# Grouped weight transfers, a hand-ordered SyncE queue and a new attention timetable in a three-stage mixer kernel

## The chip, the cores and the metric

The kernel runs on one core of a Trainium2 chip. The metric is the device time of one execution in microseconds; the time of a kernel is the median of its runs. One further execution was profiled, and all rows below are of that one.

## The reference: what is computed

Eight batches of 576 tokens go through three layers, all in float32:

```
scores = q_c @ k_c^T / 8            # 8 heads of 64, blocks of 64 tokens
attn   = softmax(scores);  x = attn @ v_c
h = relu(x^T @ w_tok1) @ w_tok2;  u = x + h^T           # mix over tokens, 576 -> 256 -> 576
x = u + relu(u @ w_ch1) @ w_ch2                         # feed-forward, 512 -> 1536 -> 512
h = relu(x @ w_in); u, v = halves of h                  # 512 -> 2 x 512
v = (v - mean) / sqrt(var + 1e-6)
out = (u * (w_spatial @ v + b)) @ w_out                 # mix over tokens, then 512 -> 512
```

## The kernel before

Every large product is made of three float16 products (high times high, high times low, low times high), so PE (TensorE) has some 10,900 matmuls. In the feed-forward, `ch1_fast` (first half, from batch 2 on) and `ch2_fast` (second half, from batch 3 on) multiply 2x2 blocks with seven products instead of eight. Their weights don't fit on the chip: each product of six matmuls takes one piece of 128 KB from DRAM (`c1s`, `c2s`). A ring of 18 slots (`call`) holds the pieces; after each product `next_piece` calls `stream`, which issues the transfers of all pieces whose slots are free. A batch has 42 pieces for either half.

The order of a batch b from 3 on: `ch1_fast` (seven rounds p, with the output products `proj` of batch b-1 between them), `ch2_fast`, `tok1` on batch b+1 (it needs that batch's attention, in `x16`), the gate stage (`gate_v`, `gate`), `tok2` of batch b+1, and the spatial products (`gated`). No stage of batch b hides attention by itself: the attention of the next batches is cut into five groups g (four of 128 tokens, one of 64), and each group into steps that are dropped in between the matmuls.

The timetable of these steps is `TIMES`, in units: step s of group g is due at 10g + s. `pump` is called after each matmul. It advances `clock` by the matmul's length, and `slow` by the same times a pace (`PACES`, by stage), and it lets a due step issue its instructions. `attention_from` makes a unit 2.04 us of `slow` (102,000 ns over 50 units). A step that is behind its due time follows the one before it after 0.6 of their distance. `BEHIND` holds two steps back further: the score matmuls (step 10) come at least 3.0 us of `clock` after `qk_lo` (5.5), and `attend` (28) at least 7.0 us after `p_lo` (20.5). Inside the rounds 0 to 5 of `ch1_fast` `held` keeps both of them, and what stands behind them, from issuing except at the end of a round without `proj`. `next_tokens` issues whatever of the next batch's attention is left before `tok1`.

The steps of a group: load of q and k (four DMAs, `at_load_qk`), `qk_hi` on ACT and `qk_lo` on DVE (the float16 halves), `score` on PE (line 245), `top`, `shift` on DVE, `expo` on ACT, `total`, `norm` on DVE, `p_hi` on ACT (line 274), `p_lo` on POOL (line 277), which also issues a transposing DMA of the probabilities into `pT` (line 278), `v_hi`, `v_lo`, `attend` on PE (line 295), `x_out` on ACT, and `x_lo` on POOL (line 314), which issues a second transposing DMA into `x16` (line 315; of the 64-token group from `xht`, which the last four matmuls of `tok1`, line 520, read).

All DMAs are issued by SP (SyncE). From batch 2 on, the instructions of PE, ACT, DVE and POOL run in the order in which the program writes them (`manual_schedule`); those of SP stand in the order in which the scheduler of the tile framework put them. In either case SP takes them one at a time: one that waits holds back those behind it. `after` postpones a function by some us of `clock`.

```
return {0: lambda: at_load_qk(g), 4: qk_hi, 5.5: qk_lo, 10: score, 10.2: lambda: wide_v(b, 2 * i, vals), 11: top, 11.8: shift,
        14: expo, 16: total, 17.5: norm, 18.8: v_hi, 19: p_hi, 19.8: v_lo, 20.5: p_lo, 28: attend, 29: x_out, 30.5: x_lo}
```

Of the kernel before, what the change touches and what calls it, by code (L numbers as in the profile page):

```python
# [27 lines left out]
def mixer_kernel(ctx: ExitStack, tc, qk0, qk, v, wt1, wt2, wc1, wc2, win, wsp, bsp, wout, out):  # L28
# [59 lines left out]
    SLOTS = 18  # L88
    A11, A12, A22, S1, S2, S3, S4 = range(7)
    ORDER1 = [n for p in range(7) for n in ((p, A11), (p, S2), (p - 1, S4), (p - 1, A22), (p, S1), (p, S3), (p, A12)) if 0 <= n[0] < 6]  # L90
# [126 lines left out]
    def at_load_qk(g):  # L217
        b, i, n = geo(g)
        for r in range(2):
            for s in range(2):  # L220
                c0 = i * 1024 + r * 4 * n
                SP.dma_start(out=qk32[half[r], s, :, 0:n],
                             in_=qk[b, half[s], c0:c0 + 4 * n].rearrange("p (h t) -> p h t", h=4))

    def at_steps(g):
        b, i, n = geo(g)
        rows, nc_, m = slice(0, n), n // 64, {}
        xT = xTs[b % 2]
        vals, v16 = v32[:, g % 2, 0:nc_], v16s[:, :, 0:nc_]
        tk = slice(i * 128, i * 128 + n)  # L230

        def qk_hi():
            ACT.activation(out=qk16[:, 0, :, :, rows], in_=qk32[:, :, :, rows], func=AF.Copy)  # L233

        def qk_lo():
            DVE.tensor_tensor(out=qk16[:, 1, :, :, rows], in0=qk32[:, :, :, rows], in1=qk16[:, 0, :, :, rows], op=ALU.subtract)  # L236

# [181 lines left out]

    TIMES = [0, 4, 5.5, 10, 10.2, 11, 11.8, 14, 16, 17.5, 18.8, 19, 19.8, 20.5, 28, 29, 30.5]  # L420
    live = {}
# [17 lines left out]
    held, told = [False], {}  # L439
    BEHIND = {10: (5.5, 3000.0), 28: (20.5, 7000.0)}  # L440

# [110 lines left out]
    def first_sums(ps, m, x):  # L552
        t1, t2 = slice(0, 288), slice(288, 576)
        xm = two(x[:, m])
        DVE.scalar_tensor_tensor(out=xm, in0=ps, scalar=DN10, in1=xm, op0=ALU.mult, op1=ALU.add)  # L555
        s = t1 if m < 2 else slice(0, 576)
        ACT.activation(out=xb[:, 0, m, s], in_=x[:, m, s], func=AF.Copy)
        after(1.4, lambda: DVE.tensor_tensor(out=xb[:, 1, m, s], in0=x[:, m, s], in1=xb[:, 0, m, s], op=ALU.subtract))  # L558
# [65 lines left out]

    def slot(i):
        return call[:, i % SLOTS * 512:i % SLOTS * 512 + 512]
# [16 lines left out]
    def sum_steps(stage, p, q):  # L643
# [16 lines left out]
        def join():  # L660
            DVE.tensor_tensor(out=f, in0=w[:, 0], in1=w[:, 1], op=ALU.add)  # L661
            for n, (k, c) in ((A11, (0, 0)), (A12, (2, 0)), (A22, (2, 128))):
                for e in range(2):
                    if stage == 1:
                        SP.dma_start(out=c1s[p, :, 512 * n + 256 * e:512 * n + 256 * e + 256].rearrange("p (k m) -> p k m", k=2),
                                     in_=w[:, e, k:k + 2, c:c + 128])
                    elif q == 0:
                        at = (p // 2) * 512 + e * 256 + p % 2 * 128
                        SP.dma_start(out=c2s[:, n, :, at:at + 128].rearrange("q p m -> p q m"),
                                     in_=c2w[:, e, 2 * p + k // 2].rearrange("p (q m) -> p q m", q=2)[:, :, c:c + 128])  # L670

        def first():
            POOL.tensor_tensor(out=s[:, 0], in0=a21, in1=a22, op=ALU.add)  # L673
            POOL.tensor_tensor(out=s[:, 2], in0=a11, in1=a21, op=ALU.subtract)

        def second():
            POOL.tensor_tensor(out=s[:, 1], in0=s[:, 0], in1=a11, op=ALU.subtract)
            POOL.tensor_tensor(out=s[:, 3], in0=a12, in1=s[:, 1], op=ALU.subtract)

# [3 lines left out]
        def low():  # L683
            DVE.tensor_tensor(out=g[:, :, 1], in0=s, in1=g[:, :, 0], op=ALU.subtract)
            if stage == 1:
                SP.dma_start(out=c1s[p, :, 1536:3584], in_=room[:, 0:2048])
# [40 lines left out]
    def ch1_fast(full, between):  # L727
# [16 lines left out]
        def sums_of(p, c):  # L744
# [15 lines left out]

            after(0.7, second)
            after(1.3, lambda: put(xp[:, 2:4], 1))
            after(1.6, others)
            after(3.0, lambda: put(t13, 3))
            after(3.6, lambda: put(t24, 5))

        for p in range(7):
            pace[0] = PACE["first" if p < 1 else "pair" if p < 5 else "turn"]
            if p < 6:
# [3 lines left out]
                ACT.activation(out=s1b[0], in_=a[:, 0, 0:288], func=AF.Copy)  # L773
                after(0.4, lambda a=a, u=u2b[p % 2]: DVE.tensor_tensor(out=u, in0=a[:, 1, 0:288], in1=s1b[0], op=ALU.add))  # L774
            if p:
# [35 lines left out]
    def ch2_fast(x):  # L811
# [14 lines left out]
        def put(t, m, cols, eng):  # L826
            hi, lo = (xb[:, e].rearrange("p m t -> p (m t)")[:, m * 576 + cols.start:m * 576 + cols.stop] for e in range(2))
            if cols.stop - cols.start > 288:
                hi, lo = two(hi), two(lo)
            ACT.activation(out=hi, in_=t, func=AF.Copy)  # L830
            eng.tensor_tensor(out=lo, in0=t, in1=hi, op=ALU.subtract)

        def tail_copy(m):
            after(3.6, lambda: DVE.tensor_copy(out=xt[:, m], in_=xb[:, :, m, 512:576]))

# [91 lines left out]
    def gate_v(j, ps=None):  # L927
# [25 lines left out]
        def finish():  # L953
# [5 lines left out]
            else:  # L959
                ACT.activation(out=vn[0:64, 8], in_=t[0:64], func=AF.Copy)  # L960
                after(1.0, lambda: DVE.tensor_tensor(out=vn[64:128, 8], in0=t[0:64], in1=vn[0:64, 8], op=ALU.subtract))

        start = 0.8 if j < 4 else 2.2
        after(start, spread_of)
        after(start + 2.0, newton)
        if exact[0]:
            after(start + 2.2, finish)
            return None
# [23 lines left out]
    def gated(m, b, eng):  # L992
        t = spatial(m)
        late = 2.2 if m == 3 else 0.0
        after(late, lambda: DVE.tensor_tensor(out=t, in0=t, in1=two(uall[:, m]), op=ALU.mult))
# [8 lines left out]

        after(late + 1.0, high_low)

# [8 lines left out]
    def store(ps, b, i, o=None, vector=False):  # L1015
# [7 lines left out]
        r0 = b * S + c0 - 64  # L1023
        SP.dma_start(out=out[r0:r0 + 128, :], in_=o)

# [40 lines left out]
    with tc.manual_schedule(engines={ET.PE}), ExitStack() as ordered:  # L1066
# [18 lines left out]
        for b in range(B):  # L1085
# [94 lines left out]
        for pair in ((0, 1), (2, 3), (4,)):  # L1180
            for i in pair:
                proj_part(banks[i], B - 1, i, (3,))
            for i in pair:
                store(banks[i], B - 1, i, hall.bitcast(F32)[:, i * DM:(i + 1) * DM], i % 2 == 1)


# [48 lines left out]
```

## Time and profile before

| | |
|---|---|
| runs, us | 1162.89, 1161.26, 1157.24 (median 1161.26) |
| the profiled execution, us | 1157.5; its span 1155.7 |
| PE busy | 1090.7 us, 94% of the span |
| DVE, ACT, POOL busy | 772.0, 496.0, 440.1 us |
| granted clock of PE, mean | 0.989 |
| bytes moved, DMA packets | 148.36 MB, 191,818 |

A row of a timeline gives the start in us from the span's start, the length, the engine, the line, what was written from what, how many such instructions were merged, and in brackets how long the engine stood idle before it and what ended that. A row of waits says which instruction waited for which, for how many us in all, how often, and the longest. A granted clock of 1.00 is 2.4 GHz, of 0.50 is 1.2 GHz. In SP's timeline the length is that of the issue, not of the transfer.

### The profile page before, as it was taken

To read this page: it belongs to the slowest core of one execution; us is meant where nothing else is said; L and a number is where in the kernel's file an instruction comes from. 1 tells how busy PE (TensorE), PEld (TensorE's weight loads), DVE (VectorE), ACT (ScalarE), POOL (GpSimd) and SP (SyncE) were. 2 spreads that over 40 slices of the span, in tenths; PEclk is the share of its full clock that TensorE was granted. 3 is DMA by queue.
4 is the path that set the end of the run, shared out by engine and by line. 5 is a ranking of instruction groups with operands and counts; after the bars stand their busy time and mean duration, and the time that the engine had idled before them with its cause. 6 is when DMAs were issued, how large, how long until landed. Compare 5 with 4: busy or idle time off the path is not lost.

```text
span 1155.7 us, 26608 instructions
## 1 busy us (share of the span) xinstructions
PE 1090.7 (94%) x10860; PEld 771.9 (67%) x10860; DVE 772.0 (67%) x1311; ACT 496.0 (43%) x890; POOL 440.1 (38%) x416
## 2 busy tenths in 40 slices
PE   5898999999999899999899997999889999999998
PEld 4576757776676675766567674777657777677765
DVE  6999977556455677776578654786658765476342
ACT  3334443434335444464244642456334562346231
POOL 0001033434244554654235451366333554255321
PEclk9899999999999999999999999999999999999999
DMA  9488730456126563257722567225762448015401
GB/s 318 141 240 267 220 94 19 120 131 154 24 60 183 129 149 83 58 149 190 203 55 57 165 174 189 56 78 150 204 155 42 129 141 219 2 56 156 128 1 46
DMA packets 191818, 148.36 MB, mean 128 GB/s; under 512 B 107344, under 2 KB 175696, under 8 KB 189392
## 3 DMA queue, kind: packets, MB, share of 16 engines
q1 hardware_dynamic: 191696, 146.66, 46.3%
q8 instruction: 85, 1.39, 0.5%
q14 instruction: 37, 0.30, 0.1%
HBM read 112.00 MB, written 20.45 MB: 115 GB/s over the span
## 4 chain that ended last, share of the span: by engine, by line
PE 36%; DVE 11%; DMA 4%; ACT 4%; POOL 3%; issue 3%; SPq 1%; ACTq 0%; DVEq 0%; POOLq 0%
PE mp L712 19%; PE mp L493 6%; PE mp L1012 5%; PE mp L924 3%; DMA pT<-p 2%; DVE xb L558 1%; DVE qk L236 1%; PE mp L516 1%; DMA x<-xht 1%; DVE vt L954 1%; DVE e L950 1%; DVE st L943 1%; POOL y L947 1%; DVE xT L555 1%; PE mp L295 1%
## 5 line engine op out<-in xcount | busy, mean ns | idle before, releaser
L712 PEld LDWEIGHTS <-c1w 128*128 128x128 f16 x2772 | 269.9, 98 | 84.3 <-issue 10.3
L712 PE MATMUL mp<-xb,c1w 128*128 128x288 f16 x864 | 129.1, 286 | 3.7 <-DVE vn L774 3.0
L898 PE MATMUL mp<-hb,c2w 128*128 128x288 f16 x864 | 110.7, 286 | 4.8 <-DVE c2w L167 3.3
L493 PE MATMUL mp<-spw,vn 128*128 128x288 f16 x896 | 111.2, 286 | 0.0
L493 PEld LDWEIGHTS <-vn 128*128 128x128 f16 x896 | 87.6, 98 | 22.3
L898 PEld LDWEIGHTS <-c2w 128*128 128x128 f16 x864 | 82.6, 98 | 27.3 <-DVE c2w L167 4.6
L493 PE MATMUL mp<-xb,inw 128*128 128x288 f16 x768 | 99.0, 286 | 0.0
L1012 PE MATMUL mp<-otw,gb 128*128 128x512 f16 x432 | 98.3, 379 | 0.0
L712 PE MATMUL mp<-hb,c1w 128*128 128x288 f16 x630 | 92.4, 291 | 3.5 <-ACT vn L840 2.2
L924 PE MATMUL mp<-inw,xb 128*128 128x512 f16 x384 | 91.1, 390 | 2.5 <-ACT xb L582 2.5
L712 PE MATMUL mp<-c2w,c1w 128*128 128x288 f16 x630 | 91.9, 288 | 0.0
L493 PEld LDWEIGHTS <-inw 128*128 128x128 f16 x768 | 74.8, 98 | 23.8
L493 PE MATMUL mp<-xb,c1w 128*128 128x288 f16 x576 | 74.9, 290 | 4.4 <-DVE xb L576 2.5
L947 POOL TENSOR_TENSOR y<-z,mhalf 128x1 f32<-128x1 f32 (+1 forms) x40 | 29.7, 743 | 124.0 <-DVE z L946 124.0
L1012 PEld LDWEIGHTS <-gb 128*128 128x128 f16 x432 | 42.2, 98 | 45.2
L493 PEld LDWEIGHTS <-c1w 128*128 128x128 f16 x576 | 56.2, 99 | 20.6 <-issue 2.9
L924 PEld LDWEIGHTS <-xb 128*128 128x128 f16 x384 | 37.6, 100 | 47.0 <-issue 4.0
L1000 POOL TENSOR_TENSOR gb<-gt,gb 128x576 f16<-128x576 f32 x31 | 43.2, 1398 | 58.0 <-ACT gb L999 58.0
L712 PE MATMUL mp<-c1w 128*128 128x288 f16 x432 | 64.7, 286 | 0.0
L236 DVE TENSOR_TENSOR qk<-qk,qk 128x1024 f16<-128x1024 f32 (+1 forms) x30 | 38.4, 1280 | 36.3 <-ACT qk L233 36.1
L958 POOL TENSOR_TENSOR vn<-vt,vn 128x512 f16<-128x512 f32 x32 | 37.8, 1180 | 55.3 <-ACT vn L957 55.3
L673 POOL TENSOR_TENSOR xs<-xs 128x128 f32<-128x128 f32 x12 | 11.6, 967 | 114.7 <-DVE xs L661 114.7
(232 smaller groups left out, 2002.3 us busy)
## 6 DMA issues: line engine op xcount, KB each, us to landing
c1w<-c1s SPq DMA_DIRECT2D x252, 128.0 KB, 2.5
c1w<-c2s SPq DMA_DIRECT2D x210, 128.0 KB, 2.5
qk<-in_qk SPq DMA_DIRECT2D x96, 128.0 KB, 2.9
out<-o SPq DMA_DIRECT2D x31, 256.0 KB, 2.0
v<-in_v SPq DMA_DIRECT2D x56, 128.0 KB, 3.0
vn<-in_wc SPq DMA_DIRECT2D x4, 1024.0 KB, 4.9
otw<-in_wc SPq DMA_DIRECT2D x3, 1024.0 KB, 5.0
spw<-in_wc SPq DMA_DIRECT2D x3, 1024.0 KB, 5.2
```

What stands on the lines that cost most here:

```text
L236: DVE.tensor_tensor(out=qk16[:, 1, :, :, rows], in0=qk32[:, :, :, rows], in1=qk16[:, 0, :, :, rows], op=ALU.subtract)
L295: PE.matmul(out=av[half[e], r, x0:x0 + 64], lhsT=v16[half[r], x, c, h], rhs=pt[half[r], y, h, 64 * c:64 * c + 64], start=(k == 0), stop=(k ...
L493: PE.matmul(out=o, lhsT=l, rhs=r, start=(i == 0), stop=(i == len(seq) - 1))
L516: PE.matmul(out=pss[m], lhsT=l, rhs=r, start=(i + j == 0), stop=False)
L673: POOL.tensor_tensor(out=s[:, 0], in0=a21, in1=a22, op=ALU.add)
L712: PE.matmul(out=o[:, 0:288], lhsT=w[:, a, k], rhs=b(e, k), start=(start and k + i == 0), stop=(stop and k == 1 and i == 2), skip_group_che ...
L898: PE.matmul(out=o, lhsT=c2w[:, a, k, mc], rhs=hb[:, k // 2, r, k % 2 * 2 + t], start=(k + e == 0), stop=(k == 11 and e == 2))
L924: PE.matmul(out=ps, lhsT=l, rhs=r, start=(k + e == 0), stop=(k == 3 and e == len(seq) - 1))
L947: POOL.tensor_tensor(out=y[0:n], in0=z[0:n], in1=mhalf[0:n], op=ALU.pow)
L958: POOL.tensor_tensor(out=vn[:, 2 * j + 1], in0=t, in1=vn[:, 2 * j], op=ALU.subtract)
L1000: eng.tensor_tensor(out=gl, in0=t, in1=gh, op=ALU.subtract)
L1012: PE.matmul(out=ps, lhsT=gb[:, l, k, tk], rhs=otw[:, r, k], start=(k == 0 and e == 0), stop=(k == 3 and e == 2))
```

## The change

- **Transfers grouped.** The pieces in DRAM are laid out in the order of use (`AT1` for the first half), and `stream` issues up to three neighbours in one transfer (`together`), when all their slots are free and they don't wrap around the ring.
- **q and k.** A group's load is two DMAs of 128 rows in place of four of 64 rows; `qk_hi` and `qk_lo` read the same elements through another view.
- **SP in program order.** From batch 2 on SP is in `manual_schedule` too.
- **Timetable.** New times for all steps; the two transposing DMAs become steps of their own, `p_turn` and `x_turn`; new distances in `BEHIND`.
- **Delays and paces.** The delays of `after` become a list `LAGS`, most with the values that they had. Three differ: 1.4 becomes 2.2 us (low half of `tok2`'s result), 3.6 becomes 2.8 us (`tail_copy`), and the DMA of an output tile comes 1.5 us after its copy is issued. Some paces change by up to 0.2.

```diff
-    A11, A12, A22, S1, S2, S3, S4 = range(7)
+    A11, A12, A22, S2, S4, S1, S3 = range(7)
+    AT1 = {A11: 0, S2: 1, S4: 2, A22: 3, S1: 4, S3: 5, A12: 6}
...
-            for s in range(2):
-                c0 = i * 1024 + r * 4 * n
-                SP.dma_start(out=qk32[half[r], s, :, 0:n],
-                             in_=qk[b, half[s], c0:c0 + 4 * n].rearrange("p (h t) -> p h t", h=4))
+            c0 = i * 1024 + r * 4 * n
+            SP.dma_start(out=one_qk[half[r]].rearrange("p (s c) -> p s c", s=2)[:, :, 0:4 * n],
+                         in_=qk[b, :, c0:c0 + 4 * n].rearrange("(s p) c -> p s c", s=2))
...
             POOL.tensor_tensor(out=p_hl[rows, 1], in0=m["sd"][rows], in1=p_hl[rows, 0], op=ALU.subtract)
+
+        def p_turn():
             SP.dma_start_transpose(out=pT[:, :, rows], in_=p16[rows].rearrange("p h r k -> p (h r k)"))
...
+        def x_turn():
             SP.dma_start_transpose(out=m["dst"].rearrange("p (k d) -> p k d", d=128), in_=m["src"])
...
-        return {0: lambda: at_load_qk(g), 4: qk_hi, 5.5: qk_lo, 10: score, 10.2: lambda: wide_v(b, 2 * i, vals), 11: top, 11.8: shift,
-                14: expo, 16: total, 17.5: norm, 18.8: v_hi, 19: p_hi, 19.8: v_lo, 20.5: p_lo, 28: attend, 29: x_out, 30.5: x_lo}
+        return {0: lambda: at_load_qk(g), 7: qk_hi, 8.2: qk_lo, 10.9: score, 11: lambda: wide_v(b, 2 * i, vals), 11.5: top, 12.1: shift, 13.2: expo, 14.6: total,
+                14.8: norm, 18.1: v_hi, 16.2: p_hi, 19.6: v_lo, 17.2: p_lo, 18: p_turn, 23.7: attend, 25.1: x_out, 26: x_lo, 27.2: x_turn}
...
-    BEHIND = {10: (5.5, 3000.0), 28: (20.5, 7000.0)}
+    BEHIND = {10.9: (8.2, 500.0), 23.7: (18, 5300.0)}
...
+    LAGS = (2.2, 0.7, 1.3, 1.6, 3, 3.6, 0.4, 2.8, 0.8, 2.2, 2, 2.2, 1, 2.2, 0, 1, 1.5, 0, 0)
     PACES = ({"first": 0.2, "pair": 0.8, "ch1": 1.0, "ch2": 1.3, "gate": 1.0, "tok1": 1.0, "last": 0.3, "turn": 0.8},
-             {"first": 0.0, "pair": 1.1, "ch1": 1.0, "ch2": 1.7, "gate": 1.2, "tok1": 1.0, "last": 0.0, "turn": 0.9},
-             {"first": 0.0, "pair": 0.7, "ch1": 1.0, "ch2": 1.75, "gate": 1.45, "tok1": 1.0, "last": 0.0, "turn": 0.3})
+             {"first": 0.0, "pair": 1.15, "ch1": 0.95, "ch2": 1.7, "gate": 1.15, "tok1": 1.0, "last": 0.0, "turn": 0.9},
+             {"first": 0.15, "pair": 0.65, "ch1": 1.0, "ch2": 1.65, "gate": 1.55, "tok1": 0.8, "last": 0.0, "turn": 0.25})
...
+    def place(stage, p, n, k):
+        return (stage, p, AT1[n]) if stage == 1 else (stage, 7 * p + n, k)
+
+    def together(i):
+        n = 1
+        while n < 3 and i + n < len(pieces) and (i + n) % SLOTS:
+            (a0, b0, c0), (a1, b1, c1) = place(*pieces[i]), place(*pieces[i + n])
+            if (a1, b1, c1) != (a0, b0, c0 + n):
+                break
+            n += 1
+        return n
+
     def stream(upto):
-        while streamed[0] < min(upto, len(pieces)):
+        while streamed[0] < len(pieces):
+            c = together(streamed[0])
+            if streamed[0] + c > upto:
+                break
             stage, p, n, k = pieces[streamed[0]]
-            src = c1s[p, :, 512 * n:512 * n + 512] if stage == 1 else c2s[p, n, :, 512 * k:512 * k + 512]
-            SP.dma_start(out=slot(streamed[0]), in_=src)
-            streamed[0] += 1
+            src = c1s[p, :, 512 * AT1[n]:512 * (AT1[n] + c)] if stage == 1 else c2s[p, n, :, 512 * k:512 * (k + c)]
+            SP.dma_start(out=slot(streamed[0], c), in_=src)
+            streamed[0] += c
...
-        SP.dma_start(out=out[r0:r0 + 128, :], in_=o)
+        after(LAGS[16], lambda: SP.dma_start(out=out[r0:r0 + 128, :], in_=o))
...
-                ordered.enter_context(tc.manual_schedule(engines={ET.Activation, ET.DVE, ET.Pool}))
+                ordered.enter_context(tc.manual_schedule(engines={ET.Activation, ET.DVE, ET.Pool, ET.SP}))
```

## Rows read from the trace of the kernel before

**Rows 1.** The page: the span, and each engine's busy time.
```profile
span 1155.7 us, 26608 instructions
...
PE 1090.7 (94%) x10860; PEld 771.9 (67%) x10860; DVE 772.0 (67%) x1311; ACT 496.0 (43%) x890; POOL 440.1 (38%) x416
```

**Rows 2.** Windows of four batches, PE alone: length, busy (count), granted clock, DMA.
```profile
434.92:573.44 138.52, 128.82 (x1324) 1.00 0.51 134
573.44:716.48 143.04, 134.44 (x1336) 0.98 0.49 130
716.48:853.37 136.89, 130.00 (x1325) 0.99 0.49 130
853.37:984.09 130.72, 129.72 (x1241) 1.00 0.50 129
```

**Rows 3.** Waits of PE, whole span: total us, times, longest us.
```profile
PE mp L295 <- DMA pT<-p: 13.5, 6, 4.2
...
PE mp L520 <- DMA x<-xht: 5.8, 4, 3.0
```

**Rows 4.** Timeline of SP's queue, end of a batch's feed-forward: start, us, instruction.
```profile
697.50 1.00 SPq L632 DMA_DIRECT2D c1w<-c1s  x2
698.55 0.47 SPq L222 DMA_DIRECT2D qk<-in_qk  x1
699.12 0.54 SPq L632 DMA_DIRECT2D c1w<-c1s  x1
699.75 1.27 SPq L315 DMA_TRANSPOSE x<-xh  x1
701.11 1.25 SPq L278 DMA_TRANSPOSE pT<-p  x1
...
713.45 1.22 SPq L315 DMA_TRANSPOSE x<-xht  x1
```

**Rows 5.** Timeline of POOL, the same stretch.
```profile
692.68 1.15 POOL L277 TENSOR_TENSOR p<-sd,p 64x512 f16<-64x512 f32 x1
```

**Rows 6.** Timeline of PE: the attend that waits, and a score of the gate stage.
```profile
590.13 0.58 PE L245 MATMUL mp<-qk 64*64 64x64 f16 x48
...
704.30 0.51 PE L295 MATMUL mp<-pT,v 64*64 64x64 f16 x24 [4.15 <-DMA pT<-p]
```

**Rows 7.** Timeline of SP's queue in the last batch that carries attention.
```profile
953.54 5.53 SPq L632 DMA_DIRECT2D c1w<-c2s  x11
```

**Rows 8.** Windows around two waits of 3 to 4 us, PE alone.
```profile
570.00:580.00 10.00, 7.04 (x26) 0.83 0.61 155
580.00:590.00 10.00, 10.00 (x114) 1.00 0.19 54
...
700.00:710.00 10.00, 5.85 (x98) 0.83 0.82 200
```

**Rows 9.** DMA issues of the page: count, KB each, median us to landing.
```profile
c1w<-c2s SPq DMA_DIRECT2D x210, 128.0 KB, 2.5
...
vn<-in_wc SPq DMA_DIRECT2D x4, 1024.0 KB, 4.9
...
pT<-p SPq DMA_TRANSPOSE x30, 3.2
```

**Rows 10.** Timeline of DVE: one group's steps, and a first step in the gate stage.
```profile
543.98 1.23 DVE L236 TENSOR_TENSOR qk<-qk,qk 128x1024 f16<-128x1024 f32 x1 [3.21 <-ACT qk L233]
545.12 0.67 DVE L263 TENSOR_REDUCE mx<-sd 64x8 f32<-64x512 f32 x1
...
546.25 0.68 DVE L269 TENSOR_TENSOR sd<-sd,mx 64x512 f32<-64x512 f32 x1
...
594.88 0.67 DVE L251 TENSOR_REDUCE mx<-mp 128x8 f32<-128x512 f32 x1
```

**Rows 11.** Timeline of ACT: the rounding of a group's probabilities.
```profile
550.00 0.62 ACT L274 ACTIVATE p<-sd 64x512 f16<-64x512 f32 x1
```

More of the change, by code (lines that the diff above doesn't have):

```diff
@@ L228, in at_steps @@
         xT = xTs[b % 2]
+        raw = one_qk.rearrange("p (s c) -> p s c", s=2)[:, :, 0:4 * n].rearrange("p s (h t) -> p s h t", h=4)
         vals, v16 = v32[:, g % 2, 0:nc_], v16s[:, :, 0:nc_]
@@ L232, in qk_hi @@
         def qk_hi():
-            ACT.activation(out=qk16[:, 0, :, :, rows], in_=qk32[:, :, :, rows], func=AF.Copy)
+            ACT.activation(out=qk16[:, 0, :, :, rows], in_=raw, func=AF.Copy)
         def qk_lo():
-            DVE.tensor_tensor(out=qk16[:, 1, :, :, rows], in0=qk32[:, :, :, rows], in1=qk16[:, 0, :, :, rows], op=ALU.subtract)
+            DVE.tensor_tensor(out=qk16[:, 1, :, :, rows], in0=raw, in1=qk16[:, 0, :, :, rows], op=ALU.subtract)
         def score():
@@ L557, in first_sums @@
         ACT.activation(out=xb[:, 0, m, s], in_=x[:, m, s], func=AF.Copy)
-        after(1.4, lambda: DVE.tensor_tensor(out=xb[:, 1, m, s], in0=x[:, m, s], in1=xb[:, 0, m, s], op=ALU.subtract))
+        after(LAGS[0], lambda: DVE.tensor_tensor(out=xb[:, 1, m, s], in0=x[:, m, s], in1=xb[:, 0, m, s], op=ALU.subtract))
         b11, b12, b21, b22 = x[:, 0:2, t1], x[:, 0:2, t2], x[:, 2:4, t1], x[:, 2:4, t2]
@@ L664, in join @@
                     if stage == 1:
-                        SP.dma_start(out=c1s[p, :, 512 * n + 256 * e:512 * n + 256 * e + 256].rearrange("p (k m) -> p k m", k=2),
+                        SP.dma_start(out=c1s[p, :, 512 * AT1[n] + 256 * e:512 * AT1[n] + 256 * e + 256].rearrange("p (k m) -> p k m", k=2),
                                      in_=w[:, e, k:k + 2, c:c + 128])
@@ L672, in first @@
         def first():
-            POOL.tensor_tensor(out=s[:, 0], in0=a21, in1=a22, op=ALU.add)
-            POOL.tensor_tensor(out=s[:, 2], in0=a11, in1=a21, op=ALU.subtract)
+            POOL.tensor_tensor(out=s[:, 2], in0=a21, in1=a22, op=ALU.add)
+            POOL.tensor_tensor(out=s[:, 3], in0=a11, in1=a21, op=ALU.subtract)
         def second():
-            POOL.tensor_tensor(out=s[:, 1], in0=s[:, 0], in1=a11, op=ALU.subtract)
-            POOL.tensor_tensor(out=s[:, 3], in0=a12, in1=s[:, 1], op=ALU.subtract)
+            POOL.tensor_tensor(out=s[:, 0], in0=s[:, 2], in1=a11, op=ALU.subtract)
+            POOL.tensor_tensor(out=s[:, 1], in0=a12, in1=s[:, 0], op=ALU.subtract)
         def high():
@@ L685, in low @@
             if stage == 1:
-                SP.dma_start(out=c1s[p, :, 1536:3584], in_=room[:, 0:2048])
+                SP.dma_start(out=c1s[p, :, 512:3584].rearrange("p (j x) -> p j x", j=2)[:, :, 0:1024],
+                             in_=room[:, 0:2048].rearrange("p (j x) -> p j x", j=2))
             else:
@@ L759, in put @@
                 made.add((p, n))
[L761 to L765, printed above, removed]
+            after(LAGS[1], second)
+            after(LAGS[2], lambda: put(xp[:, 2:4], 1))
+            after(LAGS[3], others)
+            after(LAGS[4], lambda: put(t13, 3))
+            after(LAGS[5], lambda: put(t24, 5))
         for p in range(7):
@@ L773, in ch1_fast @@
                 ACT.activation(out=s1b[0], in_=a[:, 0, 0:288], func=AF.Copy)
-                after(0.4, lambda a=a, u=u2b[p % 2]: DVE.tensor_tensor(out=u, in0=a[:, 1, 0:288], in1=s1b[0], op=ALU.add))
+                after(LAGS[6], lambda a=a, u=u2b[p % 2]: DVE.tensor_tensor(out=u, in0=a[:, 1, 0:288], in1=s1b[0], op=ALU.add))
             if p:
@@ L829, in put @@
                 hi, lo = two(hi), two(lo)
-            ACT.activation(out=hi, in_=t, func=AF.Copy)
-            eng.tensor_tensor(out=lo, in0=t, in1=hi, op=ALU.subtract)
+            after(LAGS[17], lambda: ACT.activation(out=hi, in_=t, func=AF.Copy))
+            after(LAGS[17] + LAGS[18], lambda: eng.tensor_tensor(out=lo, in0=t, in1=hi, op=ALU.subtract))
         def tail_copy(m):
-            after(3.6, lambda: DVE.tensor_copy(out=xt[:, m], in_=xb[:, :, m, 512:576]))
+            after(LAGS[7], lambda: DVE.tensor_copy(out=xt[:, m], in_=xb[:, :, m, 512:576]))
         def p1(q):
@@ L960, in finish @@
                 ACT.activation(out=vn[0:64, 8], in_=t[0:64], func=AF.Copy)
-                after(1.0, lambda: DVE.tensor_tensor(out=vn[64:128, 8], in0=t[0:64], in1=vn[0:64, 8], op=ALU.subtract))
-        start = 0.8 if j < 4 else 2.2
+                after(LAGS[12], lambda: DVE.tensor_tensor(out=vn[64:128, 8], in0=t[0:64], in1=vn[0:64, 8], op=ALU.subtract))
+        start = LAGS[8] if j < 4 else LAGS[9]
         after(start, spread_of)
-        after(start + 2.0, newton)
+        after(start + LAGS[10], newton)
         if exact[0]:
-            after(start + 2.2, finish)
+            after(start + LAGS[11], finish)
             return None
@@ L993, in gated @@
         t = spatial(m)
-        late = 2.2 if m == 3 else 0.0
+        late = LAGS[13] if m == 3 else LAGS[14]
         after(late, lambda: DVE.tensor_tensor(out=t, in0=t, in1=two(uall[:, m]), op=ALU.mult))
@@ L1003, in high_low @@
                 eng.tensor_copy(out=gb[:, 1, m, 0:64], in_=gb[:, 1, m, 576:640])
-        after(late + 1.0, high_low)
+        after(late + LAGS[15], high_low)
     def proj_part(ps, b, i, ks):
@@ L1184, in mixer_kernel @@
                 store(banks[i], B - 1, i, hall.bitcast(F32)[:, i * DM:(i + 1) * DM], i % 2 == 1)
+        settle()
 def _lay(i):
```

6 lines of the change are left out of this document (3 added, 3 removed).

## The prediction

> **What bounds the kernel now.** The page comes first: PE is busy for 1090.7 of 1155.7 us [rows 1], so at most 65 us are to be had without taking matmuls away, and the change takes none away. Next I cut the span into batches, each from the end of `tok1` to the next [rows 2]. The reader is to compare the second and the fourth window: both hold the same products (five `proj` tiles each) and differ in 95 score matmuls, since the fourth has no later batch to start on. The second takes 143.04 us with 8.6 us idle, the fourth 130.72 us with 1.0 us idle. So the stages themselves run almost without a gap; what costs time in the first three windows (9.7, 8.6 and 6.9 us idle) is something that the fourth doesn't have. The waits of PE say where it sits [rows 3]: `attend` for the transposed probabilities, 13.5 us in six waits, and the last matmuls of `tok1` for the transposed 64-token group, 5.8 us in four. The other reasons are many and short.
>
> Why are the transposes late? I followed the longest wait, 4.15 us before the `attend` at 704.30 [rows 6]. POOL had finished `p_lo` at 692.68 + 1.15 = 693.8 us [rows 5], but SP issued the transpose at 701.11, 7.3 us later [rows 4]. Meanwhile SP was not waiting: each issue begins some 0.1 us after the one before it, 0.5 us for a weight piece, 0.5 us for a load of q or k, 1.25 us for a transpose [rows 4]. SP's own issue time is the bound there. The arithmetic agrees. A piece feeds six matmuls, by `pump` 6 x (288/2.4 + 2.5) ns = 0.735 us. A batch that is behind does a group in 7.0 us (`BEHIND`) + 2.5 units (28 to 30.5) x 0.6 x 2.04/1.75 us = 8.8 us in `ch2_fast`. In these SP has to issue 12 pieces x 0.5 + 4 loads of q and k x 0.5 + 2 of v at the same 0.5 + 2.5 for two transposes = 11.5 us. It falls behind by 2.7 us a group, and the transposes, which stand at the end, carry all of that. In the fourth window there are no loads of q and k left, and eleven pieces go out in 5.5 us in one stretch [rows 7].
>
> A long wait has a second price. In the two 10 us stretches that hold waits of 3 to 4 us the granted clock is 0.83, and 1.00 right after [rows 8]. Of the two levels, 1.2 and 2.4 GHz, the lower one then holds for a third of the stretch, which costs 1.7 us of work each. It shows in the busy time too: 134.44 us against 129.72 us [rows 2], of which the 95 score matmuls at some 12 ns explain 1.1.
>
> **Transfers grouped, q and k in two.** Counted from the order of use and the ring's wrap, 462 transfers of pieces become 186; a full batch has 14 in place of 42 for `ch2_fast`. The group above then needs about 4.5 x 0.5 + 2 x 0.5 + 2 x 0.5 + 2.5 = 6.8 us of SP. Its own length is 5.3 us + 4.3 units (23.7 to 28) x 0.6 x 2.04/1.65 = 8.5 us. SP goes from 130% to 80%, and the backlog should vanish. The price of a transfer of 384 KB isn't in this trace: 128 KB land after 2.5 us, 1024 KB after 4.9 us [rows 9], so between 2.5 and 4.9 us; in proportion, 3.2 us. That is hidden: a triple goes out 15 products, 11 us, ahead of its use. A transpose that stands behind one lands after 3.2 us [rows 9], or up to 0.7 us later. I take 0.3.
>
> **SP in program order.** The stream's issues wait for products that PE has passed at that point, and what the program writes later waits behind them; so a transpose goes out where the program puts it, if POOL is done. Behind an issue that waits on a slow DVE or ACT (a load of q and k waits for `qk_lo`, an output for its copy) all others wait; the ring covers 11 - 3.2 = 8 us of that, and the latest DVE step that I found was 3.4 us behind (below). Cost: nothing up to 8 us, then one for one.
>
> **The timetable.** What goes away: `x_lo` and `p_lo` of two groups were due at the same unit (30.5 and 10 + 20.5), and with them their transposes; now they are 1.2 units apart. What gets tighter: from `total` to `attend` there were 4.5 units x 0.6 x 2.04/1.75 + 7.0 = 10.2 us in a batch that is behind; now there are 3.4 units x 0.74 + 5.3 = 7.8 us. The chain needs 1.8 us from `total` to the end of `norm` [rows 10], 0.6 for `p_hi` [rows 11], 1.15 for `p_lo` [rows 5] and 3.2 for the transpose [rows 9], 6.8 us, or 7.1 with the 0.3 above. It fits with 0.7 us to spare; I take 0.1 us for each of some ten groups that come at that speed, 1 us. From `qk_lo` to `score` the distance falls to 2.7 units; `qk_lo` takes 1.23 us [rows 10]. In `ch2_fast` 2.7 x 0.74 = 2.0 us are enough. In the gate stage it is 2.7 x 2.04/1.55 = 3.6 us, and there DVE is behind: the first step after the score of 590.13 [rows 6] was due 1 unit (1.4 us) later and started at 594.88 [rows 10], 3.4 us late. By as much `qk_lo` would be late; PE waits 3.4 + 1.2 - 3.6 = 1.0 us, once in each of three batches: 3 us. Bounds: nothing, if DVE is on time; 3 us each, 9 us, if it is as late as that and `qk_hi` on ACT as well. What waits behind `score` is all of PE.
>
> **Delays, paces, new layout.** The same instructions; the output DMAs go out 1.5 us later, at a place where SP waited for their copies anyway. Nothing before the last batch's end, where the order alone changes. I cost them at zero, with 2 us either way.
>
> **The sum.** Of 13.5 + 5.8 = 19.3 us of late transposes I take 17 as gone and one short wait of either kind as left, where `next_tokens` issues everything at once. Clock: two stretches x 1.7 = 3.4 us. Against that 1 + 3 us. Net 16.4 us off the profiled execution's 1157.5 us: **1141 us**. That execution is like the fastest of the three runs; the median is 3.8 us above it, and the forecast may be missed by that much. A difference of 0.5%, 6 us, is about what can be told from no change.
>
> **The rivals.** *Nothing is given back* (0.25). The first three windows come down to the fourth's 1.0 us of idle time: 9.7 + 8.6 + 6.9 - 3 = 22.2 us, and 3.4 us of clock: 1132 us. For it speaks that the fourth window runs so; against it the tighter distances.
>
> *Fewer issues save nothing* (0.14): the transposes are late for POOL or for the DMA engines, and only the timetable acts. Against it stands the 7.3 us between POOL's end and the issue. Then 19.3 us of waits stay, less 2.3 x 2 for the two coinciding units, and 4 us come on top: within 1 us of before, 1155 to 1162 us. The Trainium skill ("DMA: Bandwidth & Descriptors", section "Issuing engines are not separate DMA queues") speaks for this one: it calls the sequencer's time to initiate a DMA usually small relative to the DMA itself. One piece fits that, 0.5 us of issue against 2.5 us to landing; the trace disagrees as to the sum, since SP issues without a pause, and by that rule the kernel would stay at 1157 us.
>
> *DVE sets the scores' time* (0.08), the one on the other side. If DVE is late not once a batch but at most of the 25 groups, each `score` waits. At 1.5 us each, 22 groups, that is 33 us against 20.4 gained: some 1170 us. It decides from 20.4/22 = 0.9 us per group on. For it speaks the lateness of 3.4 us in the gate stage; against it that `qk_lo` gets two more units after its load, and that the fourth window's feed-forward shows no such wait.
>
> **Chances and range.** The forecast has 0.53, from 1134 to 1149 us. Faster by over 0.5% are the forecast, the first rival, and 0.04 of the second: 0.82. The rest of the second is no change, 0.10, and the third slower, 0.08. The range goes from 1126 (the first rival with 2 us from the paces and the rest of the short waits) to 1159 us, into the second rival's middle; outside are the third, half of the second and the lowest edge.
>
> **What the changed kernel's profile would show.** Right, if SP's timeline in the feed-forward has pauses, a transpose starts within 2 us of the end of `p_lo`, the waits of `attend` and `tok1` for transposes are under 4 us in sum, and the clock's two dips are gone. Wrong, if `attend` waits as before with SP idle (second rival), if the line of `score` heads PE's waits (third), or if matmuls wait for the stream: then SP in program order held the ring up for over 8 us.

## The result and the profile after

The changed kernel takes 1130.69 us in the median of four runs (1129.87 to 1133.31), the kernel before 1159.25 us (1156.68 to 1162.89, four runs): a ratio of 0.9755, interval 0.972 to 0.9791. The profiled execution of the changed kernel is the slowest of these four, 1133.31 us, 24.2 us less than that of before (1157.5 us). The prediction said 1141 us, from 1126 to 1159 us.

The page of the changed kernel, the span and the busy times:

```profile
span 1131.5 us, 25919 instructions
...
PE 1084.6 (96%) x10860; PEld 771.1 (68%) x10860; DVE 784.6 (69%) x1311; ACT 499.6 (44%) x890; POOL 441.5 (39%) x416
```

PE is busy 6.1 us less than in [rows 1] with the same 10,860 matmuls, and idle for 46.9 us in place of 65.0 us. The four windows that answer to [rows 2], each from the end of one `tok1` to the next (length, busy and count, granted clock, DMA):

```profile
432.23:566.78 134.55, 128.72 (x1325) 1.00 0.58 149
566.78:699.49 132.71, 130.42 (x1338) 1.00 0.54 137
699.49:829.05 129.56, 127.67 (x1326) 1.00 0.53 140
829.05:959.71 130.66, 129.67 (x1290) 1.00 0.48 131
```

They were 138.52, 143.04, 136.89 and 130.72 us long. The first three, which carry a later batch's attention in full, lose 4.0, 10.3 and 7.3 us; the fourth, which was nearly free of gaps, keeps its length. The second now needs 132.71 us against the fourth's 130.66 us for the same products and 48 more score matmuls. The first three together are 21.6 of the 24.2 us. Of the rest 3.6 us are won before batch 2 (see "Batch 0" below), and batch 2 gives 0.9 us back. PE's waits over the span (us in all, times, longest) answer to [rows 3]:

```profile
PE mp L246 <- DVE qk L237: 3.7, 3, 1.9
PE mp L298 <- DMA pT<-p: 3.4, 3, 1.9
...
PE mp L734 <- DVE vn L796: 2.6, 3, 1.2
...
PE mp L298 <- ACT sd L260: 1.7, 1, 1.7
```

`attend` waits 3.4 us for transposes, not 13.5; the wait of `tok1` for the 64-token group, 5.8 us before, is gone. New near the head, behind the 8.5 us for the first loads (8.7 us before), are the scores' waits for `qk_lo`, 3.7 us. None of these three lies in the gate stage: they stand at 391.15, 668.70 and 931.0 us, in the second half of the feed-forward of batches 2, 4 and 6. SP's queue in the feed-forward of batch 4, which answers to [rows 4]:

```profile
674.00 1.81 SPq L653 DMA_DIRECT2D c1w<-c2s  x2
676.41 1.29 SPq L320 DMA_TRANSPOSE x<-xh  x1
677.80 0.52 SPq L653 DMA_DIRECT2D c1w<-c2s  x1
678.43 1.19 SPq L281 DMA_TRANSPOSE pT<-p  x1
680.38 2.25 SPq L222 DMA_DIRECT2D qk<-in_qk  x2
682.73 0.55 SPq L653 DMA_DIRECT2D c1w<-c2s  x1
```

Here the issues don't follow each other without a break: 0.6 us are free before 676.41, 0.8 us before 680.38. POOL in the same place, the `p_lo` that the transpose at 678.43 waits for:

```profile
676.35 1.15 POOL L278 TENSOR_TENSOR p<-sd,p 64x512 f16<-64x512 f32 x1
```

It ends at 677.50, and its transpose is issued 0.9 us later; in [rows 4, 5] it took 7.3 us. The same stretch on PE, three of its waits:

```profile
668.70 0.53 PE L246 MATMUL mp<-qk 64*64 64x64 f16 x22 [0.86 <-DVE qk L237]
...
673.43 0.57 PE L298 MATMUL mp<-pT,v 64*64 64x64 f16 x48 [1.15 <-DMA pT<-p]
...
684.92 0.38 PE L298 MATMUL mp<-pT,v 64*64 64x64 f16 x24 [0.27 <-DMA pT<-p]
```

What is left of each is 0.3 to 1.2 us. At the ends of these feed-forwards the granted clock had fallen to 0.83 [rows 8]; now it stays at 1.00, as two windows of 10 us show:

```profile
565.00:575.00 10.00, 10.00 (x99) 1.00 0.43 100
690.00:700.00 10.00, 10.00 (x64) 1.00 0.84 200
```

The kernel before has three more windows of this kind, 50 to 60, 150 to 160 and this one:

```profile
838.00:848.00 10.00, 7.04 (x109) 0.83 0.83 205
```

They stay at 1.00 in the changed kernel too. But one dip is new there, in batch 2, where the kernel before is at 1.00 (385 to 395 us). It stands behind the longest of the scores' waits:

```profile
391.15 0.54 PE L246 MATMUL mp<-qk 64*64 64x64 f16 x44 [1.85 <-DVE qk L237]
```

```profile
390.00:400.00 10.00, 8.85 (x142) 0.83 0.73 162
```

The repeat of the changed kernel has the same wait and the same dip; the two kernels below that hold copies back have the wait without the dip, so a wait of this length does not always bring one.

The page's list of DMA issues shows the grouping (count, KB, median us to landing):

```profile
c1w<-c2s SPq DMA_DIRECT2D x70, 384.0 KB, 3.6
c1w<-c1s SPq DMA_DIRECT2D x72, 256.0 KB, 3.2
qk<-in_qk SPq DMA_DIRECT2D x49, 256.0 KB, 4.3
```

A transfer of 384 KB lands after 3.6 us (of `c1s` after 3.3 us); the prediction took 3.2 us, in proportion between the 2.5 and 4.9 us of [rows 9].

### The profile page after: what moved, and what is told of

It reads as the page before. It is cut to its first block, busy times and chain, and to the rows that moved or that the text cites. A ratio compares the mean times of both kernels' runs of the same rounds, so it can differ in the third digit from the quotient of the medians.

```text
span 1131.5 us, 25919 instructions
## 1 busy us (share of the span) xinstructions
PE 1084.6 (96%) x10860; PEld 771.1 (68%) x10860; DVE 784.6 (69%) x1311; ACT 499.6 (44%) x890; POOL 441.5 (39%) x416
## 2 busy tenths in 40 slices
DMA packets 147270, 148.30 MB, mean 131 GB/s; under 512 B 95825, under 2 KB 108113, under 8 KB 144849
## 4 chain that ended last, share of the span: by engine, by line
PE 70%; DVE 17%; ACT 3%; issue 3%; POOL 3%; DMA 3%; SPq 0%; DVEq 0%; POOLq 0%; ACTq 0%
PE mp L734 23%; PE mp L498 21%; PE mp L1034 7%; PE mp L946 6%; PE mp L920 6%; PE mp L521 3%; DVE gb L159 2%; DVE gb L155 2%; PE mp L246 1%; DVE gb L153 1%; PE mp L298 1%; DVE c L802 1%; DMA hb<-in_qk 1%; DMA c2s<-xs 1%; DMA pT<-p 1%
## 5 line engine op out<-in xcount | busy, mean ns | idle before, releaser
L946 PE MATMUL mp<-inw,xb 128*128 128x512 f16 x384 | 87.5, 379 | 1.8 <-ACT xb L588 1.6
L969 POOL TENSOR_TENSOR y<-z,mhalf 128x1 f32<-128x1 f32 (+1 forms) x40 | 26.7, 667 | 104.7 <-DVE z L968 104.7
L498 PE MATMUL mp<-t2w,hb 128*128 128x288 f16 x384 | 49.1, 286 | 1.8 <-ACT hb L1012 0.8
```

The costliest lines, as they stand in the source:

```text
L498: PE.matmul(out=o, lhsT=l, rhs=r, start=(i == 0), stop=(i == len(seq) - 1))
L946: PE.matmul(out=ps, lhsT=l, rhs=r, start=(k + e == 0), stop=(k == 3 and e == len(seq) - 1))
L969: POOL.tensor_tensor(out=y[0:n], in0=z[0:n], in1=mhalf[0:n], op=ALU.pow)
```

## Experiments

Each of the three parts was taken alone and left out alone. Grouping is the transfers of two or three pieces with q and k in two loads; order is SP in program order with the output DMA 1.5 us later; timetable is the steps' times, `BEHIND`, the paces and the delays. Ratios are to the kernel before on the same chip. The edits are shown, cut to the lines that matter, as differences from the changed kernel: a part that is left out goes back to what it was before.

| kernel | parts | median us | ratio (interval) |
|---|---|---|---|
| e1_group | grouping | 1139.17 | 0.9836 (0.9809 to 0.9862) |
| e2_order | order | 1165.49 | 1.008 (1.0053 to 1.0106) |
| e3_time | timetable | 1146.74 | 0.9909 (0.9878 to 0.9941) |
| e4_no_time | grouping, order | 1138.14 | 0.9835 (0.9808 to 0.9862) |
| e5_no_group | order, timetable | 1145.92 | 0.9907 (0.9891 to 0.9924) |
| e6_no_order | grouping, timetable | 1135.29 | 0.9815 (0.9792 to 0.9838) |
| e12_again | all three | 1130.51 | 0.9772 (0.9748 to 0.9795) |

**Grouping alone.**

```diff
-                ordered.enter_context(tc.manual_schedule(engines={ET.Activation, ET.DVE, ET.Pool, ET.SP}))
+                ordered.enter_context(tc.manual_schedule(engines={ET.Activation, ET.DVE, ET.Pool}))
...
-    BEHIND = {10.9: (8.2, 500.0), 23.7: (18, 5300.0)}
+    BEHIND = {10: (5.5, 3000.0), 28: (20.5, 7000.0)}
```

(and the times, paces and delays of before)

> Grouping alone (weight pieces in transfers of two or three, q/k of a group in two), SP's order and the timetable as before. Issue theory (SP's own issue time makes the transposes late): the waits for transposes fall from 19.3 us to under 6 us and the time to some 1140 us. Rival 'order or timetable' (issue time doesn't matter): the waits stay above 15 us, the time within 5 us of before, 1155 to 1162 us.

1139.17 us, as the issue theory said. PE's waits for transposes:

```profile
PE mp L298 <- DMA pT<-p: 5.9, 5, 1.6
...
PE mp L533 <- DMA x<-xht: 2.4, 2, 1.4
```

That is 8.3 us where there were 19.3, somewhat more than the 6 us expected. From the end of each `p_lo` to the start of its transpose's issue, taken from the trace group by group, the 24 groups of batches 3 to 7 behind the first have 2.2 us on the mean before, and 7.3 us at most; with the grouping alone 0.3 us, and 1.5 us at most; in the changed kernel 0.4 us, and 2.1 us at most. The first group of batch 3 is left out, because its `attend` comes 40 us and more after its transpose; in the changed kernel that transpose goes out 46.4 us after its `p_lo`, and PE doesn't wait for it.

**Program order alone.**

```diff
-        while n < 3 and i + n < len(pieces) and (i + n) % SLOTS:
+        while n < 1 and i + n < len(pieces) and (i + n) % SLOTS:
```

(q and k in four loads, timetable of before)

> SP in program order alone (with the output DMA 1.5 us later), pieces and q/k in single transfers, the timetable as before. Issue theory: SP still has more to issue than it has time for in the second half of the feed-forward, but the backlog is shared by the stream, which has 11 us in hand; the waits for transposes fall by about half, the time to some 1150 us. Rival 'order' (what counts is where the scheduler put the transposes): waits under 6 us, 1138 to 1142 us. Rival 'queue is held up': over 1165 us, with matmuls that wait for the stream.

1165.49 us, 0.8% slower than before: neither the issue theory nor the rival "order". The time is that of the third, "queue is held up", but without its sign, since no matmul waits for the stream. PE's waits:

```profile
PE mp L299 <- DMA pT<-p: 21.5, 11, 4.5
PE mp L534 <- DMA x<-xht: 9.7, 4, 3.4
```

31.2 us in place of 19.3. SP's queue at the end of a feed-forward shows why; note that each row begins where the one before it ends:

```profile
706.20 1.27 SPq L321 DMA_TRANSPOSE x<-xh  x1
707.56 1.22 SPq L282 DMA_TRANSPOSE pT<-p  x1
708.87 6.37 SPq L662 DMA_DIRECT2D c1w<-c1s  x12
715.33 2.42 SPq L223 DMA_DIRECT2D qk<-in_qk  x4
717.85 0.53 SPq L662 DMA_DIRECT2D c1w<-c1s  x1
718.43 1.28 SPq L349 DMA_DIRECT2D v<-in_v  x2
719.81 1.23 SPq L321 DMA_TRANSPOSE x<-xht  x1
```

The transpose of the 64-token group, at 719.81, comes behind 13 pieces, four loads of q and k and two of v that went out since the transpose before it. The thought put down for this run, that the backlog would be shared by the stream, was wrong: a transpose that stands in order behind all pieces written before it is as late as they are, and the mean from `p_lo` to its issue grows to 2.9 us. Batch 2 alone grew by 8.7 us (from the end of one `tok1` to the next, 132.4 us against 123.7); in program order 30 of the 36 copies that are spoken of below go out in it and just behind it.

**Timetable alone.**

```diff
-                ordered.enter_context(tc.manual_schedule(engines={ET.Activation, ET.DVE, ET.Pool, ET.SP}))
+                ordered.enter_context(tc.manual_schedule(engines={ET.Activation, ET.DVE, ET.Pool}))
...
-        while n < 3 and i + n < len(pieces) and (i + n) % SLOTS:
+        while n < 1 and i + n < len(pieces) and (i + n) % SLOTS:
```

(q and k in four loads, the output DMA without its delay)

> Timetable, delays and paces alone; single transfers, SP in the scheduler's order. Issue theory: SP is as late as before and the distances are shorter, so the waits for transposes grow by 2 us or more for each of some ten groups: 1165 to 1180 us. Rival 'timetable' (the two coinciding steps made the transposes late): the waits fall under 6 us, 1138 to 1145 us.

The issue theory's number fell, by 18 us and in its sign: 1146.74 us, 0.9% faster. The waits for transposes shrank:

```profile
PE mp L526 <- DMA x<-xht: 6.5, 2, 4.8
PE mp L299 <- DMA pT<-p: 6.4, 5, 3.5
```

They are 12.9 us, more than the rival's 6 us, and two of them still last 3.5 and 4.8 us. From `p_lo` to the transpose's issue it is 1.9 us on the mean, and 9.4 us at most: hardly better than the 2.2 and 7.3 us of before. What did fall is the number of SP's issues in the second half of a feed-forward, from the first matmul on `hb` to `tok1`. In batch 4 there are 59 before, with 36.3 us of issue time in 43.6 us, and here 51, with 30.6 us in 40.9 us: one load of q or k, one transpose, two loads of v and four pieces fewer. In batch 5 there are 57 and 49, in batch 3 55 and 53. The batches go the same way: batch 4 takes 138.6 us in place of 143.0 and batch 5 130.1 in place of 136.9, while batch 3 gains nothing (139.5 us against 138.5). So the new times do more of a group's steps outside of this half. That this is what the timetable gains by agrees with these counts, but isn't shown: no run changes them alone.

**Grouping and order, without the timetable; order and timetable, without the grouping; grouping and timetable, without the order.** The edits are those above, one or two at a time.

> Grouping and program order, with the timetable, delays and paces of before. Issue theory: SP is relieved and every distance is the old one, so nothing is given back at the scores: waits for transposes under 4 us, the time 1130 to 1138 us, no more than 5 us from the changed kernel's 1130.7 us. Rival 'timetable': over 1145 us.

> The changed kernel with single transfers again (462 pieces, four loads of q and k a group), program order and new timetable kept. Issue theory: SP's issues don't fit again, and in program order each late issue holds all others: waits for transposes over 10 us, 1148 to 1156 us. Rival (the timetable carries the rest of the gain by itself): under 1140 us.

> The changed kernel with SP in the scheduler's order again (outputs without the 1.5 us), grouping and new timetable kept. Issue theory: with SP relieved its order matters little: 1129 to 1135 us. Rival (the order is needed for the new distances): waits for transposes over 8 us, over 1140 us.

Without the timetable 1138.14 us, without the grouping 1145.92 us, without the order 1135.29 us. Set beside the runs with one part and with all three (0.9772), this tells what a part is worth in each company (the ratios come from three chips, each to the kernel before on its own). The grouping gives 1.6% alone, 0.9% beside the timetable, 2.5% beside the order and 1.4% beside both. The timetable gives 0.9% alone, 1.7% beside the order, 0.2% beside the grouping (the intervals overlap) and 0.6% beside both. The order costs 0.8% alone, is worth nothing beside the grouping (0.9836 and 0.9835) or beside the timetable (0.9909 and 0.9907), and gives about 0.4% beside both (the intervals of 0.9815 and 0.9772 just touch). Without the timetable the time was expected up to 5 us from the changed kernel's and lies 7.5 us off; without the grouping it is 2 us under the expected range, without the order at its upper edge.

**Issues or row length?** Grouping changes two things, the count of issues and the length of a row in DRAM (1 KB to 3 KB). Two kernels part them. In the first, a group goes out in as many parts as it has pieces, cut by rows, and q and k in four loads:

```diff
-            SP.dma_start(out=slot(streamed[0], c), in_=src)
+            cuts = {1: (0, 128), 2: (0, 64, 128), 3: (0, 48, 96, 128)}[c]
+            for r0, r1 in zip(cuts, cuts[1:]):
+                SP.dma_start(out=slot(streamed[0], c)[r0:r1], in_=src[r0:r1])
```

> The changed kernel, but each grouped transfer is issued in as many parts as it has pieces, cut by rows (48, 48 and 32 of the 128, each row still up to 3 KB), and q and k in four loads again. Issues as many as before the change, lengths of the rows as after it. Issue theory (the count of issues is what costs): like the kernel with single transfers, 1146 to 1156 us, transposes issued 2 us and more after the end of p_lo on the mean. Rival (longer rows move faster through the DMA engines, and that is the gain): 1129 to 1134 us.

1153.01 us, ratio 0.9979 (0.9963 to 0.9994): nearly all is lost again, more than with single transfers of whole pieces (0.9907), and from `p_lo` to the transpose's issue it is 2.4 us on the mean again, as expected. An issue of 48 rows takes as long as one of 128 or longer (0.42 us in the median for the parts from `c2s` and 0.48 us for those from `c1s`, against 0.38). In all, 462 issues of pieces take 227 us here and 192 us with whole pieces, which fits the larger loss. PE's waits for transposes, and SP's queue, full again:

```profile
PE mp L299 <- DMA pT<-p: 13.6, 6, 3.3
...
PE mp L526 <- DMA x<-xht: 6.2, 1, 6.2
```

```profile
563.77 1.18 SPq L656 DMA_DIRECT2D c1w<-c1s  x2
565.00 1.32 SPq L341 DMA_DIRECT2D v<-in_v  x2
566.42 5.24 SPq L656 DMA_DIRECT2D c1w<-c1s  x9
571.75 1.23 SPq L321 DMA_TRANSPOSE x<-xht  x1
```

In the second, issues are as few as in the changed kernel, and rows 1 KB long (the DMAs that fill `c1s` and `c2s` write to the same layout):

```diff
-    c2s = tc.dram_tile([2, 7, 128, 1536], F16, name="c2s")
-    c1s = tc.dram_tile([6, 128, 3584], F16, name="c1s")
+    c2s = tc.dram_tile([2, 7, 3, 128, 512], F16, name="c2s")
+    c1s = tc.dram_tile([6, 7, 128, 512], F16, name="c1s")
...
-            src = c1s[p, :, 512 * AT1[n]:512 * (AT1[n] + c)] if stage == 1 else c2s[p, n, :, 512 * k:512 * (k + c)]
-            SP.dma_start(out=slot(streamed[0], c), in_=src)
+            src = c1s[p, AT1[n]:AT1[n] + c] if stage == 1 else c2s[p, n, k:k + c]
+            SP.dma_start(out=slot(streamed[0], c).rearrange("p (k m) -> p k m", m=512), in_=src.rearrange("k p m -> p k m"))
```

> The changed kernel with the grouped transfers kept, but the pieces laid out one behind the other in DRAM, so that a transfer of three reads three rows of 1 KB for each partition and not one of 3 KB. Issues as few as after the change, rows as short as before it. Issue theory: within 4 us of the changed kernel, 1128 to 1135 us. Rival (long rows are needed as well): over 1140 us.

1135.58 us, ratio 0.9811 (0.9783 to 0.984), against 0.9772 (0.9748 to 0.9795) for the changed kernel beside it. The runs don't overlap (1133.24 to 1137.26 and 1128.12 to 1131.74 us), the intervals do a little. The packets go with the rows and not with the time: 191,818 before, 184,230 in this fast kernel, 152,648 in the slow row-cut one and 147,270 in the changed kernel. So the count of issues is what the grouping is worth, and the longer rows perhaps 0.4% of it. The time is 0.6 us over the expected range; the rival's 1140 us is not reached.

**The scores' distance.**

```diff
-        return {0: lambda: at_load_qk(g), 7: qk_hi, 8.2: qk_lo, 10.9: score,
+        return {0: lambda: at_load_qk(g), 6: qk_hi, 7.1: qk_lo, 10.9: score,
```

(`TIMES` and the key of `qk_lo` in `BEHIND` likewise)

> The changed kernel with qk_hi due at 6 (not 7) and qk_lo at 7.1 (not 8.2), so that score comes 3.8 units after it and not 2.7. If PE's waits of score for qk_lo (3.7 us in three) are the price of the short distance, they fall under 1.5 us and the time by 2 to 3 us, to 1128 us. Rival (DVE has the same work in the gate stage and is as late at the next step): within 1 us of 1130.7 us, the wait found at another line.

1132.99 us, ratio 0.9794 (0.9778 to 0.9811): no gain over the changed kernel. PE's waits:

```profile
PE mp L298 <- DMA pT<-p: 4.4, 4, 1.7
...
PE mp L298 <- DVE mx L265: 2.6, 1, 2.6
...
PE mp L246 <- DVE qk L237: 1.3, 2, 0.7
```

The scores' wait fell from 3.7 to 1.3 us as expected, and with it the dip of the clock at 390 us went. But an `attend` of batch 3, which had waited 1.7 us for ACT in the changed kernel, now waits 2.6 us for DVE, transposes cost 1.0 us more, and behind that `attend` there is a dip again:

```profile
541.00:551.00 10.00, 7.91 (x95) 0.83 0.97 275
```

So the price was found at other lines, as the rival said, though the time is 2.3 us from 1130.7 and not within 1 us. Its reason, the same work of DVE in the gate stage, is not shown: all of these waits lie in the feed-forward, in different batches.

**Batch 0.** A part of the gain lies where the prediction had none. The last matmuls of `tok1` for batch 2's tokens, before and after:

```profile
311.21 1.03 PE L520 MATMUL mp<-x,t1w 128*128 128x512 f16 x4
```

```profile
307.64 1.03 PE L525 MATMUL mp<-x,t1w 128*128 128x512 f16 x4
```

3.6 us are won by then, in one traced execution of each; the repeat of the changed kernel (`e12_again`) is 0.5 us later there. In the kernels with SP in program order this point lies at 305.9 to 309.4 us, in those with the scheduler's order (but for the one below that holds copies back) at 309.4 to 311.2 us. The timeline of SP in the kernel before:

```profile
127.56 7.61 SPq L669 DMA_DIRECT2D c2s<-c2w  x12
...
139.71 0.34 SPq L134 DMA_DIRECT2D otw<-in_wsp  x1
```

The 36 copies of weights for the second half (from `c2w` to `c2s`) are written in batch 2, yet the scheduler had put them at 94 to 152 us, among the weight loads of batch 0. In program order six stay there and 30 leave. The load at 139.71 feeds ACT's conversion of `wsp`, behind which ACT and DVE do the residual that the gate stage waits for. PE there, before and after:

```profile
151.34 8.34 PE L924 MATMUL mp<-inw,xb 128*128 128x512 f16 x30 [2.52 <-ACT xb L582]
```

```profile
149.46 0.61 PE L946 MATMUL mp<-inw,xb 128*128 128x512 f16 x2 [1.58 <-ACT xb L588]
```

The wait falls from 2.5 to 1.6 us, and the matmuls behind it run at full clock (28 in 6.2 us; before, 30 in 8.3 us). The order gains 1.6 to 4.9 us up to this point in each of the four pairs of traces that differ in it. In batch 2, where most of the copies now stand, it gives back 8.7 us alone, 2.7 us beside the grouping, 1.8 us beside the timetable and 0.4 us beside both. That is part of why it is worth something only beside both; the rest lies in later batches. To test the copies' part the copies were held back in the kernel without program order:

```diff
-                        SP.dma_start(out=c2s[:, n, :, at:at + 128].rearrange("q p m -> p q m"),
-                                     in_=c2w[:, e, 2 * p + k // 2].rearrange("p (q m) -> p q m", q=2)[:, :, c:c + 128])
+                        with tc.issue_after(last_sum[0]):
+                            SP.dma_start(out=c2s[:, n, :, at:at + 128].rearrange("q p m -> p q m"),
+                                         in_=c2w[:, e, 2 * p + k // 2].rearrange("p (q m) -> p q m", q=2)[:, :, c:c + 128])
```

> SP in the scheduler's order, grouping and new timetable as in the changed kernel, but the 36 copies of second-half weights into DRAM are held behind the last sums of the first half, so that they cannot go out among the weight loads of batch 0. Theory: what program order gave with grouping and timetable was mostly that these copies left batch 0; the wait of gate_v for ACT at 149 us shrinks from 3.0 to 1.6 us or less, the dip of the granted clock there goes, and the time falls from 1135.3 us by some 3 us to that of the changed kernel. Rival (the gain was the order of the transposes in later batches): no change from 1135.3 us.

The place behaves as expected. From 140 to 160 us PE (length, busy and count, granted clock, DMA) had, without program order and without the hold,

```profile
140.00:160.00 20.00, 16.79 (x109) 0.91 0.70 187
```

and with the hold

```profile
140.00:160.00 20.00, 19.43 (x139) 1.00 0.59 162
```

so 2.6 us of work more, and no dip of the clock; the wait there is 0.4 us. The last products of `tok1` for batch 2 start at 308.5 us, against 310.8 us without the hold and 307.6 and 308.1 us in the two traces of the changed kernel. As to the whole time, 1133.52 us (1.8 us less than without the hold, where some 3 us were expected) and a ratio of 0.9797 (0.9775 to 0.9818) lie between 0.9815 without the hold and 0.9772; the intervals overlap on either side, so the measurement agrees but doesn't settle it.

> The changed kernel with the 36 copies of first-half weights (45 to 89 us) held behind the last weight load as well. If copies of short rows in front of weight loads are what makes batch 0 slow, the waits for weights before 180 us shrink further and the time falls by 1 to 3 us. Rival (DVE, 90% busy there, is the bound of batch 0): within 1 us of the changed kernel.

For this one the copies of `c1w` were held behind the last weight load in the same way. 1132.58 us, ratio 0.979 (0.977 to 0.9811): not faster than the changed kernel beside it. The gate stage's wait for ACT is gone (1.8 us in the repeat of the changed kernel), and the last products of `tok1` for batch 2 start at 306.4 us, but that doesn't show in the whole time; nor is it clearly within the rival's 1 us.

> The changed kernel itself, on the chip of the runs beside it, for their comparison: a ratio to the kernel before of 0.972 to 0.979, as at first.

0.9772 (0.9748 to 0.9795). No version here beats the changed kernel.

## Why the prediction was right, and where it was off

- **What bounds the kernel.** Right. SP's issue time in the feed-forward made the transposes late, and behind the long waits the clock fell. Grouping alone gives 1.6% of the 2.3 to 2.5%; the same bytes in as many issues as before, beside the other two parts, give 0.2%.
- **The size.** The time lies in the range, but outside the forecast's own 1134 to 1149 us: 16.4 us were to go and 24.2 us went. Of the 7.8 us between, 2.7 us are in PE's busy time and 5.1 us in its idle time. The idle time fell by 18.1 us: 15.9 us of waits for transposes, less 4.2 us that the scores give back (3.7 us for `qk_lo`, 0.5 us for `qk_hi`), and some 6.4 us of other short waits (2.0 us of them a score's wait for ACT), which the sum had put at nothing.
- **Transfers grouped.** 17 of 19.3 us of late transposes were to go; 15.9 went (3.4 us are left). The load on SP fell further than the 80% reckoned: in the second half of batch 4's feed-forward 31 issues take 20.0 of 36.5 us. A large transfer lands up to 0.4 us later than I took.
- **The clock.** 3.4 us were to come back, for two dips; PE's busy time fell by 6.1 us. From 50 us on there were five dips and now there is one, the new one in batch 2, which the sum did not have.
- **SP in program order, "cost: nothing up to 8 us".** It held up no stream, as expected, but not because an ordered queue costs nothing: alone it costs 0.8%, since a full queue in program order delays the transposes as well; beside both other parts it gives about 0.4%. I looked at the batches from 2 on, and not at what the scheduler had moved out of them into batch 0: by place, some 3 us of the 7.8 us.
- **The timetable, "1 + 3 us" given back.** The size is right by luck. The scores were to wait 1.0 us in the gate stage of each of three batches, and the feed-forward was to have room enough; the 3.7 us are all in the feed-forward's second half, behind a `qk_lo` that had itself waited 0.9 to 1.1 us for `qk_hi` on ACT, and the longest has the new dip of the clock behind it. The 1 us for `attend` can't be told from nothing: one waits 1.7 us for ACT, in the repeat of the kernel none does, and before one had waited 1.7 us for DVE. The part as a whole is no loss, but gives 0.2 to 1.7% by what stands beside it: the prediction weighed the distances within a group and didn't count where the steps' own issues fall. Its 1.2 units between two groups hold for `p_lo` and `x_lo`; their transposing DMAs are 0.8 units apart (27.2 and 10 + 18).
- **The signs.** SP's timeline has pauses, all but one of the 24 transposes start within 2 us of `p_lo` (the latest 2.1 us), their waits are 3.4 us in sum, and the two dips of [rows 8] are gone. The third rival's sign shows as well, since behind the first loads the line of `score` heads PE's waits; but these are three waits in all, not one at each group.
- **The rivals.** "Nothing is given back", 1132 us, was the nearest to the result, for another reason than the one it stated: the first three windows are idle for 10.0 us and not for 3, and the scores do give back 3.7 us; the shorter busy time and batch 0 make up for it. "Fewer issues save nothing" fell with the grouping alone and with the row-cut kernel. The Trainium skill ("DMA: Bandwidth & Descriptors", section "Issuing engines are not separate DMA queues") calls the time to initiate a DMA usually small relative to the DMA itself. For one DMA this holds here, 0.38 us against 2.5 us; the runs disagree as to a queue, where 59 issues of one engine fill 36.3 of 43.6 us and fewer issues give 1.6%. "DVE sets the scores' time" came true for single groups only.
- **What stays open.** It is open what the timetable gains by, beyond the counts above. Why the order's gain in batch 0 is kept only beside both other parts was followed into batch 2 and not further. The 0.4% between the kernels with rows of 1 KB and of 3 KB may be due to the transfers themselves or to their issues, which take 0.36 us against 0.32 us.

## What to carry to other kernels

Add up an issuing engine's own time in the stage that matters, count by duration, and compare it with the stage's length: a queue that issues without a pause is a bound like any other, and what was late here is the last thing in it, not the thing that fills it. Merging transfers helped, and so did a timetable that leaves fewer of them in the full stage; putting the full queue in program order didn't. A part's worth depends on what stands beside it, so take each alone and leave each out. When a scheduler's freedom is taken away, look also at what it had moved ahead, far from the lines that were changed.

## What was not expected of the hardware

An issue's time on SP hardly grows with the bytes: one transfer of 128 KB takes 0.38 us in the median before, one of 384 KB 0.32 us after, and a part of 48 rows costs a whole issue, 0.42 to 0.48 us. A transfer of three rows of 1 KB per partition (0.36 us) costs SP about as much as one of a single row of 3 KB (0.32 us).
